# A convolution moved from TensorE to VectorE, block transposes, and a first matmul in four 32-row tiles

## The chip, the cores and the metric

The kernel runs on one NeuronCore of one Trainium2 chip. The metric is the device time of one execution in microseconds (us). The engines named here are PE (TensorE, matmuls; PEld is its weight loads), DVE (VectorE), ACT (ScalarE), POOL (GpSimd) and SP (SyncE, which here only issues DMAs). Matmuls read SBUF and write PSUM, which has eight banks of 512 float32 per partition; DVE and ACT take the results out.

## The reference

```python
# x: (B, S, D) = (8, 4224, 192); weight: (H, K) = (8, 7); w1: (192, 768); w2: (768, 192)
w = softmax(weight, axis=-1)
x_pad = concatenate([zeros((B, K - 1, D)), x], axis=1)
out[b, s, h, g] = sum_k w[h, k] * x_pad[b, s + k, h, g]      # 8 heads of 24 channels
mu, var = mean(out), mean((out - mu) ** 2)                    # over the 192 channels
xn = (out - mu) / sqrt(var + 1e-06) * g_ln
result = out + maximum(xn @ w1, 0.0) @ w2
```

All of it is float32; w1 and w2 arrive as float64 bits and are rounded on the chip.

## The kernel before

A group is 11 tiles of 128 consecutive tokens, a third of a sequence; there are 24 groups. Tokens lie on the partitions, tile after tile. Each group goes through the MLP in three blocks of 4, 4 and 3 tiles.

`conv` makes the causal convolution a matmul. For each of 8 heads, `band` (128 x 128) mixes the tokens of one tile (L218, 264 columns: 11 tiles of 24 channels), and `halo` adds the six tokens that reach back into the tile before (L222, 64 rows by 32 columns of the array). The results go from PSUM to `y` by ACT or DVE. `norm` computes the statistics of each token and writes the normalised tile `xn` (L259) on DVE. `transpose` turns `xn` into channels-on-partitions by matmuls with an identity (L279).

`up` is the first matmul. The contraction is over 192 channels: 128 of them fill the array (L297), the other 64 use half of it. The hidden dimension comes in six chunks of 128, handled in pairs, and the two chunks' half-array matmuls lie in the two halves of the array (L303): rows 0 to 63 for one chunk, 64 to 127 for the other. ReLU is done by ACT and DVE (L307, L311) into `ht`. `down` is the second matmul, six chunks per tile (L326), and `y` is added by DVE (L330) on the way out.

A float32 matmul of the program is two PE passes, each with its own weight load, so counts in the profile are twice those of the code. Engines run their own queues in order; a scheduler fixes the order in each queue when the program is built, and semaphores do the waiting. PSUM is split into three pools: two banks for convolution and transposes, four for `up`, two for `down`. Before the loop, POOL and DVE build the band matrices and DVE converts the weights (`to_float32`).

Of the kernel before, what the change touches and what calls it, by code (L numbers as in the profile page):

```python
# [9 lines left out]
I32 = mybir.dt.int32  # L10
# [7 lines left out]
def kernel(  # L18
# [23 lines left out]
    Q = 64  # L42
    GRP = D // H
    PAD = K - 1
    T = 11
    NF = F // P
    NG = B * S // (T * P)
    GPS = S // (T * P)
    BLKS = [(0, 4), (4, 4), (8, 3)]
    NB = len(BLKS)  # L50
    HB = 32

    assert D == P + Q and S % (T * P) == 0 and T * GRP <= 512
    assert NF % 2 == 0 and PAD < HB

    xf = x.flatten_outer_dims()
    of = out.flatten_outer_dims()

    consts = ctx.enter_context(tc.tile_pool(name="consts", bufs=1))
    setup = ctx.enter_context(tc.tile_pool(name="setup", bufs=2))  # L60
    xpool = ctx.enter_context(tc.tile_pool(name="xin", bufs=3))
    ypool = ctx.enter_context(tc.tile_pool(name="y", bufs=3))
    npool = ctx.enter_context(tc.tile_pool(name="norm", bufs=3))
    hpool = ctx.enter_context(tc.tile_pool(name="hid", bufs=2))
    opool = ctx.enter_context(tc.tile_pool(name="outp", bufs=3))
    ps_c = ctx.enter_context(tc.tile_pool(name="ps_c", bufs=2, space=PSUM))
    ps_h = ctx.enter_context(tc.tile_pool(name="ps_h", bufs=4, space=PSUM))
    ps_o = ctx.enter_context(tc.tile_pool(name="ps_o", bufs=2, space=PSUM))

# [26 lines left out]
    NB1 = NF // 2 * P  # L96
    NW1 = F + NB1
    NW2 = NF * D
    w1 = consts.tile([P, NW1], F32, name="w1")
    w1a = w1[:, 0:F]  # L100
    w1b = w1[:, F:NW1].rearrange("p (c f) -> p c f", f=P)
    w2flat = consts.tile([P, NW2], F32, name="w2")
    w2 = w2flat.rearrange("p (c d) -> p c d", d=D)
    raw1 = consts.tile([P, NW1, 2], U32, name="raw1")
    raw2 = consts.tile([P, NW2, 2], U32, name="raw2")
# [5 lines left out]
    w1tail = w1_words[P:D, :].rearrange("k (c two f) -> k two c f", two=2, f=2 * P)  # L111
    nc.scalar.dma_start(out=ga, in_=g_col[0:P, :])
# [3 lines left out]
    for r in range(2):  # L116
        rows = slice(Q * r, Q * r + Q)
        nc.scalar.dma_start(out=gb[rows, :], in_=g_col[P:D, :])
        nc.scalar.dma_start(
            out=raw1[rows, F:NW1, :].rearrange("p (c f) w -> p c (f w)", f=P),  # L120
            in_=w1tail[:, r, :, :],
        )
    nc.scalar.dma_start(
# [4 lines left out]
    def to_float32(dst, raw, n):  # L128
        """dst = raw, rounded: 1.mantissa as a float32, times the signed power of two. The
        power runs from 0 (below float32's normal range) to infinity (above it)."""  # L130
        lo, hi = raw[:, :, 0], raw[:, :, 1]
        power = setup.tile([P, n], U32, tag="power", name="power", bufs=1)
        scale = setup.tile([P, n], U32, tag="scale", name="scale", bufs=1)
        mant = setup.tile([P, n], U32, tag="mant", name="mant", bufs=1)
        rest = setup.tile([P, n], U32, tag="rest", name="rest", bufs=1)
# [31 lines left out]
    ident = consts.tile([P, P], F32, name="ident")  # L167
    make_identity(nc, ident)
# [19 lines left out]
    # ---- bands: band[j, h, s] = taps[h, j - s + PAD] within a tile; halo the same with  # L188
    # j counted from the end of the tile before, where only s < PAD is reached ----
    band = consts.tile([P, H, P], F32, name="band")  # L190
    halo = consts.tile([P, H, HB], F32, name="halo")

    def build(dst, width, base):
        dist = setup.tile([P, width, K], I32, tag=f"dist{width}", name=f"dist{width}", bufs=1)
        mask = setup.tile([P, width, K], F32, tag=f"mask{width}", name=f"mask{width}", bufs=1)
        nc.gpsimd.iota(dist, pattern=[[-1, width], [-1, K]], base=base, channel_multiplier=1)
        nc.vector.tensor_single_scalar(mask, dist, 0, op=ALU.is_equal)
        for h in range(H):
            prod = setup.tile([P, width, K], F32, tag="prod", name=f"prod{width}_{h}")
            nc.gpsimd.tensor_tensor(  # L200
                prod, mask, taps[:, h : h + 1, :].to_broadcast([P, width, K]), op=ALU.mult
            )
            nc.vector.tensor_reduce(dst[:, h, :], prod, axis=AX.X, op=ALU.add)  # L203

    build(band, P, PAD)
    build(halo, HB, PAD - P)

# [1 line left out]
    y = {}  # L209

    def conv(g, h0, h1):
        if h0 == 0:
            y[g] = ypool.tile([P, T, D], F32, tag="y", name=f"y{g}")
        first = 0 if g % GPS else 1
        for h in range(h0, h1):
            cs = slice(h * GRP, h * GRP + GRP)
            pc = ps_c.tile([P, T, GRP], F32, tag="c", name=f"pc{g}_{h}")
# [8 lines left out]
            if h % 2:  # L226
                nc.vector.tensor_copy(y[g][:, :, cs], pc)  # L227
            else:
                nc.scalar.copy(y[g][:, :, cs], pc)  # L229
        if h1 == H:  # L230
            del xg[g]

    xn = {}

    def norm(n):
        g, (b0, bn) = n // NB, BLKS[n % NB]
        st = npool.tile([P, 4, nc.vector.BN_STATS_DIM], F32, tag="st", name=f"st{n}")
        mv = npool.tile([P, 4, nc.vector.BN_AGGR_DIM], F32, tag="mv", name=f"mv{n}")
        rstd = npool.tile([P, 4], F32, tag="rstd", name=f"rstd{n}")
        half = npool.tile([P, 4], F32, tag="half", name=f"half{n}")  # L240
        t = npool.tile([P, 4, 2 * P], F32, tag="xn", name=f"xn{n}")
        for i in range(bn):
            nc.vector.bn_stats(out=st[:, i, :], in_=y[g][:, b0 + i, :])  # L243
            nc.vector.bn_aggr(out=mv[:, i, :], in_=st[:, i, :])  # L244
        nc.scalar.activation(rstd[:, 0:bn], mv[:, 0:bn, 1], AF.Sqrt, bias=eps)  # L245
        nc.vector.reciprocal(rstd[:, 0:bn], rstd[:, 0:bn])
        # One Newton step, as the table of square roots is coarser than float32:
        # r (1.5 - 0.5 (var + eps) r r).
        r, v, sq = rstd[:, 0:bn], mv[:, 0:bn, 1], half[:, 0:bn]
        nc.vector.tensor_tensor(sq, r, r, op=ALU.mult)  # L250
# [3 lines left out]
        nc.vector.tensor_scalar(
            out=sq, in0=sq, scalar1=-0.5, scalar2=1.5, op0=ALU.mult, op1=ALU.add
# [141 lines left out]
```

## Time and profile before

| What | Value |
|---|---|
| Median of 3 runs | 1467.71 us (1467.4 to 1468.08) |
| Profiled execution, span | 1465.8 us |
| PE busy | 1412.3 us (96%) |
| PEld busy | 865.2 us (59%) |
| DVE busy | 499.7 us (34%) |
| ACT busy | 251.7 us (17%) |
| POOL busy | 53.8 us (4%) |
| Granted PE clock | 1.000 throughout |
| HBM | 29.13 MB read, 25.95 MB written |

The span runs from the first to the last instruction of the profiled execution; the median contains 1.9 us that lie outside it. An engine's share is an average over the span. A line with L and a number is a line of the kernel printed above.

### The profile page before, as it was taken

The page shows a single profiled execution, that of the slowest core. Times are in us where ns is not written, and L with a number is a line of the kernel's source. Part 1 is how long each engine was busy: PE and PEld are TensorE (multiplying, and loading weights), DVE is VectorE, ACT ScalarE, POOL GpSimd, SP SyncE. Part 2 cuts the span into 40 slices and gives each one's busy share as a digit, 9 for nine tenths or more (in the row PEclk, how much of TensorE's full clock was granted, in tenths as well). Part 3 has the DMA queues.
Part 4 walks back from the last instruction along what each step waited for, and adds up shares of the span by engine and source line. Part 5 has one row for each costly group of instructions (what it writes and reads, how often), then busy time and mean ns, then how long its engine had stood idle before and what let it go on. Part 6 is the DMA issues. An engine that isn't in the chain of part 4 may idle for free.

```text
span 1465.8 us, 15445 instructions
## 1 busy us (share of the span) xinstructions
PE 1412.3 (96%) x6192; PEld 865.2 (59%) x6192; DVE 499.7 (34%) x1655; ACT 251.7 (17%) x531; POOL 53.8 (4%) x96
## 2 busy tenths in 40 slices
PE   0599999999999999999999999999999999999999
PEld 0256656666566566665665666666656666666576
DVE  4723414324234143142341431433414414324141
ACT  0111111112111111111111111111111111111111
POOL 4300000000000000000000000000000000000000
PEclk9999999999999999999999999999999999999999
DMA  5101101101001011010010110110101101000000
GB/s 156 30 13 48 53 19 49 46 26 50 30 31 53 19 51 51 19 51 29 32 52 19 50 53 20 49 40 22 53 19 49 53 19 50 11 20 22 19 20 30
DMA packets 73031, 56.07 MB, mean 38 GB/s; under 512 B 3072, under 2 KB 72832, under 8 KB 72960
## 3 DMA queue, kind: packets, MB, share of 16 engines
q1 hardware_dynamic: 71312, 52.73, 11.4%
q10 hardware_dynamic: 1648, 2.36, 0.5%
q8 instruction: 49, 0.80, 0.2%
q14 instruction: 22, 0.18, 0.0%
HBM read 29.13 MB, written 25.95 MB: 38 GB/s over the span
## 4 chain that ended last, share of the span: by engine, by line
PE 96%; POOL 1%; DVE 1%; DMA 1%; issue 0%; SPq 0%; DVEq 0%
PE po L326 36%; PE ph L297 25%; PE ph L303 15%; PE pc L218 8%; PE pc L222 7%; PE pt L279 5%; POOL prod L200 1%; DMA xg<-in_x_dram 1%; DMA raw<-in_moe_w_ch_dram 0%; DVE st L243 0%; DVE mant L159 0%; DVE scale L147 0%; DVE w L165 0%; DVE mant L155 0%; DVE w L161 0%
## 5 line engine op out<-in xcount | busy, mean ns | idle before, releaser
L326 PE MATMUL po<-w,ht 128*128 128x192 f32 x3168 | 539.2, 328 | 0.0
L326 PEld LDWEIGHTS po<-w,ht 128*128 128x128 f32 x3168 | 511.9, 190 | 19.5 <-issue 19.5
L297 PE MATMUL ph<-xt,w 128*128 128x512 f32 (+1 forms) x864 | 391.3, 575 | 0.0
L307 ACT ACTIVATE ht<-ph 128x512 f32<-128x512 f32 (+1 forms) x216 | 121.6, 563 | 819.3 <-PE ph L303 819.3
L297 PEld LDWEIGHTS ph<-xt,w 128*128 128x128 f32 x864 | 150.7, 190 | 187.5 <-issue 168.4
L311 DVE TENSOR_SCALAR ht<-ph 128x512 f32<-128x512 f32 x144 | 93.2, 647 | 441.7 <-PE ph L303 441.7
L303 PE MATMUL ph<-xt,w 64*128 64x512 f32 (+1 forms) x864 | 228.5, 606 | 0.0
L330 DVE TENSOR_TENSOR ob<-po,y 128x384 f32<-128x384 f32 x144 | 75.4, 523 | 277.7 <-PE po L326 277.7
L218 PE MATMUL pc<-xg,band 128*128 128x264 f32 x384 | 141.1, 450 | 28.6 <-DVE band L203 28.5
L303 PEld LDWEIGHTS ph<-xt,w 64*128 64x128 f32 x864 | 65.0, 184 | 148.4 <-issue 147.7
L222 PE MATMUL pc<-xg,halo 64*32 64x264 f32 (+1 forms) x384 | 121.6, 398 | 11.6 <-DVE halo L203 11.6
L218 PEld LDWEIGHTS pc<-xg,band 128*128 128x128 f32 x384 | 58.7, 193 | 100.5 <-issue 60.0
L227 DVE COPY y<-pc 128x264 f32<-128x264 f32 x96 | 41.5, 433 | 189.1 <-PE pc L222 189.1
L279 PEld LDWEIGHTS pt<-ident,xn 128*128 128x128 f32 x528 | 57.0, 141 | 60.0 <-issue 59.4
L243 DVE BATCH_NORM_STATS2 st<-y 128x6 f32<-128x192 f32 x264 | 86.5, 336 | 2.4
L259 DVE TENSOR_SCALAR xn<-y,mv,rstd 128x192 f32<-128x192 f32 x264 | 82.9, 376 | 5.4 <-DVE rstd L257 0.5
L279 PE MATMUL pt<-ident,xn 128*128 128x128 f32 x528 | 74.7, 283 | 9.7 <-DVE xn L259 9.7
L268 POOL COPY xn<-xn 128x256 f32<-128x256 f32 (+1 forms) x72 | 27.7, 385 | 1328.9 <-DVE half L250 1207.4
L222 PEld LDWEIGHTS pc<-xg,halo 64*32 64x32 f32 x384 | 26.1, 106 | 80.8 <-issue 66.9
L229 ACT COPY y<-pc 128x264 f32<-128x264 f32 x96 | 36.4, 380 | 191.6 <-PE pc L222 191.6
L281 DVE COPY xt<-pt 128x512 f32<-128x512 f32 (+1 forms) x72 | 46.6, 647 | 19.0 <-PE pt L279 17.2
L245 ACT ACTIVATE rstd<-mv,eps 128x4 f32<-128x4 f32 (+1 forms) x72 | 21.5, 299 | 170.9 <-DVE mv L244 101.1
(41 smaller groups left out, 248.1 us busy)
## 6 DMA issues: line engine op xcount, KB each, us to landing
xg<-in_x_dram SPq DMA_DIRECT2D x48, 384.0 KB, 4.2
out_dram<-ob SPq DMA_DIRECT2D x48, 384.0 KB, 2.6
xg<-in_x_dram SPq DMA_DIRECT2D x24, 288.0 KB, 4.7
out_dram<-ob SPq DMA_DIRECT2D x24, 288.0 KB, 2.3
raw<-in_moe_w_ch_dram ACTq DMA_DIRECT2D x1, 1152.0 KB, 10.6
raw<-in_moe_w_ch_dram ACTq DMA_DIRECT2D x1, 768.0 KB, 9.5
xg<-in_x_dram SPq DMA_DIRECT2D x16, 48.0 KB, 2.1
raw<-in_moe_w_ch_dram ACTq DMA_DIRECT2D x2, 192.0 KB, 8.0
```

Of the source, the lines that this page charges most:

```text
L218: nc.tensor.matmul(pc, band[:, h, :], xg[g][:, 1 : T + 1, cs], start=True, stop=True, skip_group_check=True,)
L222: nc.tensor.matmul(pc[0:HB, first:T, :], halo[Q:P, h, :], xg[g][Q:P, first:T, cs], start=False, stop=True, skip_group_check=True,)
L243: nc.vector.bn_stats(out=st[:, i, :], in_=y[g][:, b0 + i, :])
L259: nc.vector.tensor_scalar(out=t[:, i, 0:D], in0=y[g][:, b0 + i, :], scalar1=mv[:, i, 0:1], scalar2=rstd[:, i : i + 1], op0=ALU.subtract, o ...
L279: nc.tensor.transpose(pt[:, i, :], xn[n][:, i, c * P : c * P + P], ident)
L281: eng(t[:, 0:bn, :], pt[:, 0:bn, :])
L297: nc.tensor.matmul(ph[r][:, 0:bn, :], w1a[:, f0 : f0 + P], xa[:, 0:bn, :], start=True, stop=False,)
L303: nc.tensor.matmul(ph[r][:, 0:bn, :], w1b[rows, c, :], xb[rows, 0:bn, :], start=False, stop=True,)
L307: nc.scalar.activation(ht[:, 2 * c, 0:bn, :], ph[0][:, 0:bn, :], AF.Relu)
L311: nc.vector.tensor_scalar(out=ht[:, 2 * c + 1, 0:bn, :], in0=ph[1][:, 0:bn, :], scalar1=0.0, scalar2=None, op0=ALU.max,)
L326: nc.tensor.matmul(po[:, i, :], ht[:, f, i0 + i, :], w2[:, f, :], start=(f == 0), stop=(f == NF - 1),)
L330: nc.vector.tensor_tensor(ob[:, i0 : i0 + m, :], po[:, 0:m, :], y[g][:, b0 + i0 : b0 + i0 + m, :], op=ALU.add,)
```

## The change

The tokens are laid out anew: partition p holds a run of 33 consecutive tokens of one sequence, and a group is 11 of these 33 on all 128 partitions (still 24 groups of 1408 tokens). The tokens before a run are loaded with it, so a tap of the convolution is a shift along the free dimension. `conv` becomes 56 DVE instructions per group, each on 128 x (11 x 24) elements: 8 that multiply by the first tap (L239 of the changed program), then 6 x 8 that multiply by a tap and add (L244). Band matrices, identity and the matmuls of `conv` and `transpose` go.

The normalisation is no longer written out. The mean is taken out of the weights: w1 has each column's mean over channels (after scaling with g) subtracted, once, before the loop (`prepare_w1`); the mean comes from four matmuls. The factor 1/std is positive, so it passes through the ReLU and is applied on the way out of `down`, in the instruction that adds `y` (L320, one for each 192 columns). `stats` computes it from bn_stats.

`transpose` is one DVE instruction that transposes every 32 x 32 block of `y` (L251): 32 channels come to lie on each 32 partitions, for the tokens of those 32 partitions. So `up` contracts 32 channels at a time: for each of six chunks of hidden and six blocks of channels (24 groups x 36 = 864 such steps), four matmuls (L297 of the changed program) whose weights and data lie on partitions 0, 32, 64 and 96, with 352 columns each and a PSUM bank each. For this w1 must lie four times on the partitions, so its centred form is written to memory and read back four times. All ReLUs are on ACT. PSUM is one pool of eight banks for everything; `ht` has one buffer, `yt` two, `y` and `xg` three. x is loaded and the output stored in rows of 8 KB and more.

```diff
-            nc.tensor.matmul(
-                pc, band[:, h, :], xg[g][:, 1 : T + 1, cs],
-                start=True, stop=True, skip_group_check=True,
-            )
-            nc.tensor.matmul(
-                pc[0:HB, first:T, :], halo[Q:P, h, :], xg[g][Q:P, first:T, cs],
-                start=False, stop=True, skip_group_check=True,
-            )
...
+xr = x.rearrange("b (p r) d -> b p (r d)", p=P)
+outr = out.rearrange("b (p r) d -> b p (r d)", p=P)
...
+    def load_x(g):
+        b, j0 = groups[g]
+        t = xpool.tile([P, J + PAD, D], F32, tag="xg", name=f"xg{g}")
...
+        if j0:
+            nc.sync.dma_start(out=flat, in_=xr[b, :, (j0 - PAD) * D : (j0 + J) * D])
+            return
...
+    def prepare_w1():
+        to_float32(w1f, raw1, NW1)
...
+            nc.tensor.matmul(mean[r][:, 0:FH], share[:, 0, :], w1f[:, fs], start=True, stop=False)
...
+            nc.vector.scalar_tensor_tensor(
+                out=w1f[:, fs], in0=w1f[:, fs], scalar=ga, in1=mean[r][:, 0:FH],
+                op0=ALU.mult, op1=ALU.subtract,
+            )
...
+        for q in range(NQ):
+            (nc.sync, nc.scalar)[q % 2].dma_start(
+                out=w1[C * q : C * q + C, :, :], in_=w1c.rearrange("(c d) f -> d c f", d=C)
+            )
...
+    def conv(g):
+        t = xg.pop(g)
+        y[g] = ypool.tile([P, J, D], F32, tag="y", name=f"y{g}")
+        for k in range(K):
+            for h in range(H):
+                cs = slice(h * GRP, h * GRP + GRP)
+                tap = taps[:, h, k : k + 1]
+                if k == 0:
+                    nc.vector.tensor_scalar(
+                        out=y[g][:, :, cs], in0=t[:, 0:J, cs], scalar1=tap, scalar2=None,
+                        op0=ALU.mult,
+                    )
+                else:
+                    nc.vector.scalar_tensor_tensor(
+                        out=y[g][:, :, cs], in0=t[:, k : k + J, cs], scalar=tap,
+                        in1=y[g][:, :, cs], op0=ALU.mult, op1=ALU.add,
+                    )
...
+    def transpose(g):
+        yt[g] = tpool.tile([P, J, NC, C], F32, tag="yt", name=f"yt{g}")
+        nc.vector.transpose(
+            yt[g].rearrange("p j c t -> p (j c t)"), y[g].rearrange("p j d -> p (j d)")
+        )
...
+    def up(g):
...
+        for f in range(NF):
+            fs = slice(f * P, f * P + P)
+            ph = [psum.tile([P, 512], F32, tag="ps", name=f"ph{g}_{f}_{q}") for q in range(NQ)]
+            for c in range(NC):
+                for q in range(NQ):
+                    rows = slice(C * q, C * q + C)
+                    nc.tensor.matmul(
+                        ph[q][:, 0:W], w1[rows, c, fs], t[rows, :, c, :],
+                        start=(c == 0), stop=(c == NC - 1),
+                    )
+            for q in range(NQ):
+                nc.scalar.activation(
+                    ht[g][:, f, :, q, :], ph[q][:, 0:W].rearrange("p (j t) -> p j t", t=C), AF.Relu
                 )
...
+            for j, dst in zip(js, at):
+                nc.vector.scalar_tensor_tensor(
+                    out=y[g][:, j, :], in0=dst, scalar=rstd[g][:, j : j + 1],
+                    in1=y[g][:, j, :], op0=ALU.mult, op1=ALU.add,
+                )
...
+    prepare_w1()
+    conv(0)
     transpose(0)
...
+    for g in range(NG):
+        if g + 2 < NG:
+            load_x(g + 2)
+        up(g)
+        if g + 1 < NG:
+            conv(g + 1)
+            transpose(g + 1)
+            stats(g + 1)
+        down(g)
```

What moves in the queues is seen at two places. First PE, in the steady part: the end of `up` of one block and what follows it (`ph`: first matmul, `pt`: transposes, `po`: second matmul, `pc`: convolution; the numbers behind the names count buffers). Before:

```order
L303 MATMUL ph_4_3494<-xt_1_3407,w_96 128x512
L303 MATMUL ph_5_3495<-xt_1_3407,w_96 128x512
L279 MATMUL pt_0_3502<-ident,xn_3430 128x128 x3
L279 MATMUL pt_1_3508<-ident,xn_3430 128x128 x3
L326 MATMUL po_0_3555<-w_97,ht_3477 128x192
L218 MATMUL pc_4_3514<-xg_3060,band 128x264
L222 MATMUL pc_4_3514<-xg_3060,halo 32x264
```

Between first and second matmul stood transposes of the next block and half a group's convolution. In the changed program, at the end of the first group's `up`:

```order
L297 MATMUL ph_5_0_411<-yt_207,w_113 128x352
L297 MATMUL ph_5_1_412<-yt_207,w_113 128x352
L297 MATMUL ph_5_2_413<-yt_207,w_113 128x352
L297 MATMUL ph_5_3_414<-yt_207,w_113 128x352
L315 MATMUL po_0_527<-w_114,ht_250 128x192 x12
L315 MATMUL po_2_542<-w_114,ht_250 128x192 x12
L315 MATMUL po_4_557<-w_114,ht_250 128x192 x12
L315 MATMUL po_6_572<-w_114,ht_250 128x192 x12
L315 MATMUL po_8_587<-w_114,ht_250 128x192 x12
L315 MATMUL po_10_602<-w_114,ht_250 128x192 x6
```

Now matmuls in four row tiles (third number of `ph`) are followed by the 66 matmuls of the group's `down`, and those by the next group's `up`, with nothing between.

Second DVE, around the instruction that combines `po` with `y`. Before, in the steady part (L311 ReLU, L281 transposes out of PSUM, L227 convolution out of PSUM, L330 adds):

```order
L311 TENSOR_SCALAR ht_1842<-ph_5_1860 128x512
L281 COPY xt_1_1879<-pt_1_1874 128x512
L227 COPY y_1881<-pc_1_1886 128x11x24
L227 COPY y_1881<-pc_3_1894 128x11x24
L330 TENSOR_TENSOR ob_1919<-po_0_1920,y_1575 128x384
L330 TENSOR_TENSOR ob_1919<-po_2_1934,y_1575 128x384
L311 TENSOR_SCALAR ht_1949<-ph_3_1959 128x512
```

Each is a short step on a PSUM tile. In the changed program, near the start (`y_809` is group 2, `po_0_527` and `y_150` are group 0; the rows ahead of these, L239 and L244, are group 2's convolution):

```order
L261 BN_STATS st_868<-y_809 128x6 x11
L264 TENSOR_TENSOR d_869<-st_868 128x11
L265 TENSOR_TENSOR v_870<-st_868 128x11
L266 SCALAR_TENSOR_TENSOR d_869<-d_869 128x11
L269 SCALAR_TENSOR_TENSOR v_870<-v_870,d_869 128x11
L251 STREAM_TRANSPOSE yt_866<-y_809 128x2112
L320 SCALAR_TENSOR_TENSOR y_150<-po_0_527,r_212,y_150 128x192 x2
L320 SCALAR_TENSOR_TENSOR y_150<-po_2_542,r_212,y_150 128x192 x2
```

The combines of group 0 (L320) now stand behind the convolution, statistics and block transpose of group 2.

## Rows read from the trace of the kernel before

**Rows 1.** The chain that ended last, by line: share of the span.
```profile
PE po L326 36%; PE ph L297 25%; PE ph L303 15%; PE pc L218 8%; PE pc L222 7%; PE pt L279 5%; POOL prod L200 1%; DMA xg<-in_x_dram 1%; DMA raw<-in_moe_w_ch_dram 0%; DVE st L243 0%; DVE mant L159 0%; DVE scale L147 0%; DVE w L165 0%; DVE mant L155 0%; DVE w L161 0%
```

**Rows 2.** Busy time of each engine in one stretch of two groups (x: instructions).
```profile
202.27:319.18 116.91, 116.91 (x518) 71.85 (x517) 38.89 (x134) 20.74 (x44) 2.31 (x6) 1.00 0.12 38
```

**Rows 3.** PE's timeline: start, length, instructions, waits in brackets.
```profile
701.80 1.56 PE L297 MATMUL ph<-xt,w 128*128 128x384 f32 x4
...
704.13 1.56 PE L297 MATMUL ph<-xt,w 128*128 128x384 f32 x4
...
707.39 6.02 PE L326 MATMUL po<-w,ht 128*128 128x192 f32 x36
713.25 1.88 PE L297 MATMUL ph<-xt,w 128*128 128x512 f32 x4
...
716.12 1.98 PE L297 MATMUL ph<-xt,w 128*128 128x512 f32 x4
...
719.09 1.98 PE L297 MATMUL ph<-xt,w 128*128 128x512 f32 x4
...
722.99 0.49 PE L326 MATMUL po<-w,ht 128*128 128x192 f32 x2
723.39 0.71 PE L218 MATMUL pc<-xg,band 128*128 128x264 f32 x2
...
724.55 0.71 PE L218 MATMUL pc<-xg,band 128*128 128x264 f32 x2
```

**Rows 4.** Timeline of one pair step: PE matmuls and PEld weight loads.
```profile
655.57 1.02 PE L297 MATMUL ph<-xt,w 128*128 128x512 f32 x2
...
656.00 0.59 PE L297 MATMUL ph<-xt,w 128*128 128x512 f32 x1
656.52 0.30 PEld L303 LDWEIGHTS ph<-xt,w 64*128 64x128 f32 x4 [0.76 <-issue]
656.52 1.13 PE L303 MATMUL ph<-xt,w 64*128 64x512 f32 x4
...
657.05 0.59 PE L303 MATMUL ph<-xt,w 64*128 64x512 f32 x2
```

**Rows 5.** Groups by form: busy us, mean ns of one, idle before.
```profile
L243 DVE BATCH_NORM_STATS2 st<-y 128x6 f32<-128x192 f32 x264 | 86.5, 336 | 2.4
L259 DVE TENSOR_SCALAR xn<-y,mv,rstd 128x192 f32<-128x192 f32 x264 | 82.9, 376 | 5.4 <-DVE rstd L257 0.5
...
L330 DVE TENSOR_TENSOR ob<-po,y 128x384 f32<-128x384 f32 x120 | 66.8, 557 | 244.3 <-PE po L326 244.3
...
L307 ACT ACTIVATE ht<-ph 128x384 f32<-128x384 f32 x72 | 35.4, 492 | 148.6 <-PE ph L303 148.6
...
L251 DVE SCALAR_TENSOR_TENSOR half<-mv,eps,half 128x4 f32<-128x4 f32 x48 | 12.3, 258 | 0.0
...
L330 DVE TENSOR_TENSOR ob<-po,y 128x192 f32<-128x192 f32 x24 | 8.6, 358 | 33.4 <-PE po L326 33.4
```

**Rows 6.** DVE's timeline while the weights are converted.
```profile
17.19 0.76 DVE L136 TENSOR_SCALAR power<-raw 128x1152 uint32<-128x1152 uint32 x1 [10.28 <-DMA raw<-in_moe_w_ch_dram]
17.87 0.75 DVE L151 TENSOR_SCALAR mant<-raw 128x1152 uint32<-128x1152 uint32 x1
...
19.21 1.35 DVE L155 SCALAR_TENSOR_TENSOR mant<-raw,mant 128x1152 uint32<-128x1152 uint32 x1
20.48 0.20 DVE L181 TENSOR_REDUCE wsum<-taps 128x8 f32<-128x56 f32 x1
```

**Rows 7.** PE's timeline at the start of the first block.
```profile
67.23 2.35 PE L279 MATMUL pt<-ident,xn 128*128 128x128 f32 x8 [9.73 <-DVE xn L259]
69.38 2.84 PE L297 MATMUL ph<-xt,w 128*128 128x512 f32 x4
```

**Rows 8.** DMA issues: count, size of each, median us to landing.
```profile
out_dram<-ob SPq DMA_DIRECT2D x24, 288.0 KB, 2.3
raw<-in_moe_w_ch_dram ACTq DMA_DIRECT2D x1, 1152.0 KB, 10.6
```

More of the change, by code (lines that the diff above doesn't have):

```diff
@@ L42 @@
     Q = 64
+    C = 32
     GRP = D // H
     PAD = K - 1
-    T = 11
+    R = S // P
+    J = 11
     NF = F // P
[L47 to L57, printed above, removed]
+    NC = D // C
+    NQ = P // C
+    W = J * C
+    assert D == P + Q and S % P == 0 and R % J == 0 and W <= 512 and NF % 2 == 0
@@ L116 @@
     for r in range(2):
-        rows = slice(Q * r, Q * r + Q)
-        nc.scalar.dma_start(out=gb[rows, :], in_=g_col[P:D, :])
         nc.scalar.dma_start(
-            out=raw1[rows, F:NW1, :].rearrange("p (c f) w -> p c (f w)", f=P),
-            in_=w1tail[:, r, :, :],
-        )
+            out=raw1[Q * r : Q * r + Q, F:NW1, :].rearrange("p f w -> p (f w)"),
+            in_=w1_words[P:D, 2 * FH * r : 2 * FH * (r + 1)],
+        )
+    nc.scalar.dma_start(out=ga, in_=g_col[0:P, :])
+    for r in range(2):
+        nc.scalar.dma_start(out=gb[Q * r : Q * r + Q, :], in_=g_col[P:D, :])
+    load_x(0)
+    load_x(1)
     nc.scalar.dma_start(
@@ L205 @@
[L205 to L217, printed above, removed]
+    w1f = setup.tile([P, NW1], F32, name="w1f")
+    w1 = consts.tile([P, NC, F], F32, name="w1")
+    w2flat = consts.tile([P, NW2], F32, name="w2")
@@ new lines @@
+    w2 = w2flat.rearrange("p (c d) -> p c d", d=D)
+    w1c = dram.tile([D, F], F32, name="w1c")
+    def prepare_w1():
+        to_float32(w1f, raw1, NW1)
+        share = setup.tile([P, 2, P], F32, name="share")
+        for i, g in enumerate((ga, gb)):
+            nc.vector.tensor_scalar(
+                out=share[:, i, :], in0=g.to_broadcast([P, P]),
+                scalar1=1.0 / D, scalar2=None, op0=ALU.mult,
+            )
+        mean = [psum.tile([P, 512], F32, tag="ps", name=f"mean{r}") for r in range(2)]
+        for r in range(2):
+            fs = slice(FH * r, FH * r + FH)
+            rows = slice(Q * r, Q * r + Q)
+            nc.tensor.matmul(mean[r][:, 0:FH], share[:, 0, :], w1f[:, fs], start=True, stop=False)
@@ L230, in conv @@
[L230 to L250, printed above, removed]
-        nc.vector.scalar_tensor_tensor(
-            out=sq, in0=v, scalar=eps, in1=sq, op0=ALU.add, op1=ALU.mult
+                mean[r][:, 0:FH], share[rows, 1, :], w1f[rows, F:NW1], start=False, stop=True
+            )
@@ new lines, in prepare_w1 @@
+        for r in range(2):
+            fs = slice(FH * r, FH * r + FH)
+            rows = slice(Q * r, Q * r + Q)
+            nc.vector.scalar_tensor_tensor(
+                out=w1f[:, fs], in0=w1f[:, fs], scalar=ga, in1=mean[r][:, 0:FH],
+                op0=ALU.mult, op1=ALU.subtract,
+            )
+            nc.vector.scalar_tensor_tensor(
+                out=w1f[rows, F:NW1], in0=w1f[rows, F:NW1], scalar=gb[rows, :],
+                in1=mean[r][rows, 0:FH], op0=ALU.mult, op1=ALU.subtract,
+            )
@@ L253, in norm @@
         )
         nc.vector.tensor_scalar(
[L255 removed]
+            out=d, in0=d, scalar1=-0.5, scalar2=1.5, op0=ALU.mult, op1=ALU.add
         )
[L257 to L266 removed]
@@ L325, in down @@
+    def down(g):
+        b, j0 = groups[g]
+        t = ht.pop(g)
+        for i0 in range(0, J, 2):
+            js = range(i0, min(i0 + 2, J))
+            po = psum.tile([P, 512], F32, tag="ps", name=f"po{g}_{i0}")
+            at = [po[:, i * D : i * D + D] for i in range(len(js))]
+            for j, dst in zip(js, at):
                 for f in range(NF):
                     nc.tensor.matmul(
-                        po[:, i, :], ht[:, f, i0 + i, :], w2[:, f, :],
+                        dst, t[:, f, j, :, :].rearrange("p q t -> p (q t)"), w2[:, f, :],
@@ L352 @@
+    conv(0)
     transpose(0)
-    for n in range(steps):
-        g, k = divmod(n, NB)
-        if k == 0 and g + 2 < NG:
+    stats(0)
+    to_float32(w2flat, raw2, NW2)
+    for g in range(NG):
+        if g + 2 < NG:
             load_x(g + 2)
-        up(n)
-        if n == 0:
-            to_float32(w2flat, raw2, NW2)
-        if n + 1 < steps:
-            transpose(n + 1)
-        if g + 1 < NG and k < 2:
-            conv(g + 1, k * H // 2, (k + 1) * H // 2)
-        if n + 2 < steps:
-            norm(n + 2)
-        down(n)
+        up(g)
[4 more added lines that the diff above has]
+        down(g)
```

191 lines of the change are left out of this document (60 added, 131 removed).

## The prediction

> **What bounds the kernel now.** I read the chain of waits first. Nearly all of it is TensorE (PE): 36% in the second matmuls (L326), 25% and 15% in the first ones (L297, L303), 8% and 7% in the convolution (L218, L222), 5% in the transposes (L279) [rows 1]. No other engine has more than 1%, so only what changes PE's own work, or makes PE wait, can move the time. Next, the stretches: two groups of 1408 tokens last 116.91 us, PE is busy in all of it and DVE in a third [rows 2], so a group costs 58.5 us of PE. PE's timeline splits this. One pass over six hidden chunks is three pair steps; a pair step of a 4-tile block repeats every 2.97 us (716.12 to 719.09), of a 3-tile block every 2.33 (701.80 to 704.13), so up() costs 6 x 2.97 + 3 x 2.33 = 24.8 us per group. 36 passes of the second matmul take 5.86 us (707.39 to 713.25), 0.163 each, so 132 of them 21.5. A head of the convolution repeats every 1.165 us (723.39 to 724.55), eight make 9.3. A 4-tile transpose takes 0.93 (719.09 + 2.97 to 722.99), a group some 2.6 [rows 3]. The sum is 58.2, against 58.5 measured.
>
> Inside a pair step the reader is to see why it costs more than its matmuls. A 512-column pass starts 0.43 us after the one before (655.57, 656.00). Then come the two half-array matmuls: four passes in two rounds, the second round of two starting at 657.05, 0.53 after the first. So two row tiles do run at once, each at full rate. But the array stood from 656.43 to 656.52, then loaded weights with nothing to hide them (0.11, the rest of the 0.53) [rows 4]. A step holds four full passes and two rounds, 6 x 0.43 = 2.58 of its 2.97 us: 0.39 goes to two changes between full array and half tiles, 0.2 each.
>
> **The change, part by part.** *PE loses* the convolution (9.3 us a group) and the transposes (2.6). *up()* becomes 36 steps (6 chunks of hidden, 6 of channels), each of four 32-row matmuls of 352 columns, each in two passes. A pass of 352 columns is 0.43 x 352/512 = 0.296 us; if the four tiles run at once, a step is 0.59 and 36 are 21.3. All neighbours have the same tile shape, so only two changes of shape remain, 0.4: 21.7 instead of 24.8. *down()* keeps its 132 passes, 21.5. A group: 43.2 us, 15.3 less than now.
>
> The row shows two tiles at once, never four, so the step is bounded by 0.59 and 1.18 us. I take 0.59: the two tiles start together and neither slows the other. The four weight loads there overlap too (0.30 us for all) [rows 4].
>
> The Trainium skill bears on this ("TensorE: Matmul & The Clock Gate", Part 3, its speedup table): packing four 32-row tiles was measured there at 3.07 times one, not four. By that a step would be 0.77 us and the estimate 155 us longer than mine. No row here has four tiles, so it stays a rival.
>
> *ACT* takes all the ReLU work: four evictions of 352 per chunk, each under 0.49 us (that of 384 columns) [rows 5], 2.0 us in the 3.5 of a chunk. Eight banks hold two chunks, so it is hidden. After the last chunk, down() has 5 x 2 passes (1.6 us) to run before it needs the last chunk's evictions; I cost this at nothing.
>
> *DVE gains* the convolution: per group 8 tensor-scalar and 48 scalar-tensor-tensor instructions of 264 elements. No row shows this form. DVE's slope is (557 - 358)/192 = 1.04 ns an element [rows 5]; a scalar-tensor-tensor of 1152 with no per-partition scalar starts its successor 1.27 us later, 0.07 over the slope, and a tensor-scalar of 1152 0.68 later, so that form takes half the slope [rows 6]. With two per-partition scalars, 192 elements are spaced 82.9/264 = 0.314 us, 0.21 over the half slope [rows 5]: 0.07 more for each scalar. So 0.275 + 0.14 = 0.415 for one of the 48 and 0.28 for one of the 8: 22.1 us per group. Bounds: 0.345 with a free scalar (18.8), and no overlap at all, 0.275 + 0.258 (the duration on 4 elements [rows 5]) = 0.53 (28).
>
> The Trainium skill says the latter ("VectorE: DVE Perf Modes", The DRAIN you can't avoid): the next instruction does not start until the pipe is empty. The row disagrees: 264 instructions of 0.376 us would be 99 us, and their busy time is 82.9 [rows 5]. By the rule the whole kernel would be some 17 us longer than my sum, through its start alone.
>
> The block transpose (2112 elements) has no row: 2.3 us at one element per slope, four times that at worst; I take 2.3, since every form here runs at the slope or better. Statistics: 11 x 0.336 = 3.7 [rows 5] and four small ones, 0.8; Newton step 1.0; 11 combines with scalar from PSUM 0.36 + 0.07, 4.7. DVE's group: 34.6 us, hidden under PE's 43.2 once the pipeline runs. x arrives two groups ahead; the bytes are about the same.
>
> *The start* is not hidden. Now the first up() begins at 69.38 us [rows 7]. In the changed program it needs yt of group 0: raw weights (17.19 now [rows 6]; all three loads are issued first now, so 11 to 17, I take 14), conversion 6 x 0.68 + 4 x 1.27 and small ones, 10 (to 24), convolution 22.1, centring of w1 2 and a wait for its mean matmuls 1, first step of w2's conversion 0.7, transpose 2.3: 52 us. w1's way through memory (0.6 MB out, 2.4 in) starts near 31; at the 1.15 MB in 10.6 us of a crowded queue [rows 8] it would end near 58: the upper bound. PE then runs up(0) and down(0): 52 + 43.2 + 2.2 for slow first matmuls (eight transposes take 2.15 instead of 0.93, the next four passes 2.84 instead of 1.88 [rows 3, 7]) = 97.5.
>
> Here the order matters. DVE has group 2's whole convolution *ahead* of the combine of group 0. From 52: rest of w2's conversion and statistics 14 (66), conv(1) 22.1, transpose (91), stats(1), conv(2), stats(2), transpose (125), and only then the combine, which frees the banks of po_0. PE's up(1) needs these banks for its third and fourth tile, so PE, done at 97.5, waits until about 125.5: 28 us, once. Afterwards DVE's 34.6 us leave the order harmless: its combine begins some 31 us into each group, when the first pair of tiles has just come out, and follows PE.
>
> **Sum.** 125.5 + 23 x 43.2 + 2.2 (restart) + last combine 0.4 + last output, 1.06 MB in one transfer, 6 (between 2.3 for 288 KB and 10.6 for 1152 KB [rows 8]) = 1127.7. The profiled execution had a span of 1465.8 us against a median of 1467.71, so add 1.9: **1130 us**, 338 less. Own range 1110 to 1165: 0.345 or 0.53 in three exposed convolutions is -10 or +17, w1's arrival +6, a slow transpose +13, early weights -3.
>
> **Rivals.**
> *Four tiles overlap only in part* (three at a time): step 0.79, +0.197 x 864 = +170: 1300. For: no row has four. Against: two cost each other nothing.
> *Only two at once* (slower): a step takes two rounds more, 1.18, +0.59 x 864 = +511: 1641. For it: two is all that rows show. It decides from a step of 0.98 us on (338/864 above 0.59). Against it: the passes of one tile already interleave with the other's, so the order within a tile doesn't hold the neighbour back.
> *Weight loads in single file*: eight a step; a load holds its rows some 0.11 us before a pass can start [rows 4]; eight in a row 0.88, +0.29 x 864 = +250: 1380. Against: the loads of the two tiles start together.
> *DVE becomes the bound*: from conv = 43.2 - 12.5 = 30.7 us, 0.55 an instruction, beyond my upper bound; strided runs of 24 elements on three operands could do it. At 0.6, a group costs 46 us, +64, and the start +34: 1228.
>
> **Chances.** Forecast 0.74; part overlap 0.08; two at once 0.06; loads in file 0.04; DVE bound 0.07; rest 0.01. A measurement tells apart some 0.2%. Faster are all but two at once: 0.93; same 0.01; slower 0.06. The range that leaves out two in ten holds the forecast and most of the DVE case: 1105 to 1230.
>
> **What would show it.** L297 in steps of four, a step every 0.59 us (0.77 or 0.79: part overlap; 0.88: loads; 1.18: two); PE's conv and pt gone; PE's period 43 us; one wait near 97 to 125 us on DVE's combine (L320), none like it later; L244 spaced 0.41; DVE near 60% busy in steady groups. PE waiting for L320 or yt in every group would mean that DVE binds and the prediction is wrong.

## The result and the profile after

| | Before | After |
|---|---|---|
| Median | 1467.86 us (1467.4 to 1468.08, 4 runs) | 1125.59 us (1125.42 to 1126.09, 4 runs) |
| Ratio, with 95% interval | | 0.7669 [0.7659, 0.768] |
| Span of the profiled execution | 1465.8 us | 1123.8 us |
| PE busy | 1412.3 us (96%) | 1048.6 us (93%) |
| DVE busy | 499.7 us (34%) | 795.2 us (71%) |
| Mean granted PE clock | 1.000 | 0.988 |

The time fell by 342 us; 338 were forecast (1130 us). The page of the changed kernel, its parts 1, 2 and 5:

```profile
PE 1048.6 (93%) x10088; PEld 872.8 (78%) x10088; DVE 795.2 (71%) x2145; ACT 230.4 (21%) x603; POOL 9.1 (1%) x12
...
PEclk9987999999999999999999999999999999999999
...
L297 PE MATMUL ph<-yt,w 32*128 32x352 f32 x6912 | 523.2, 458 | 46.4 <-ACT ht L302 24.2
...
L315 PE MATMUL po<-w,ht 128*128 128x192 f32 x3168 | 522.3, 327 | 0.0
...
L244 DVE SCALAR_TENSOR_TENSOR y<-xg,taps,y 128x264 f32<-128x264 f32 x1152 | 467.7, 485 | 0.0
```

PE is still the bound, with two lines left where there were six [rows 1]. In its whole idle time ahead of L297, 46.4 us, only two waits are large: 22.2 for the first `yt`, and 24.2 put down to ACT's evictions, which was not forecast. The granted clock (PEclk, tenths of full speed; 9 is 90% or more) falls under that in two of its 40 slices alone, the third and the fourth (56 to 112 us).

The chain of waits of the changed kernel, in order of time (start, length, what), shows the steady rhythm:

```profile
103.21 21.65 PE po L315 x132
124.86 21.51 PE ph L297 x288
```

A group lasts 21.51 + 21.69 = 43.20 us; 43.2 were forecast, against 58.5 before [rows 2]. Of the 15.3 us less, `up` gives 3.3 (24.8 to 21.51); the rest is work that left PE. Of the 288 passes in 21.51 us four run at a time: 72 rounds of 0.299, where one pass of 352 columns alone was put at 0.296 by the forecast. A step of two rounds is 0.60 us, not 0.77 and not 1.18.

DVE in one steady group (timeline of the changed kernel; start, length, line, in brackets the idle time before it and its releaser):

```profile
518.54 2.26 DVE L239 TENSOR_SCALAR y<-xg,taps 128x264 f32<-128x264 f32 x8 [2.89 <-DMA out_dram<-y]
520.72 19.48 DVE L244 SCALAR_TENSOR_TENSOR y<-xg,taps,y 128x264 f32<-128x264 f32 x48
540.23 2.96 DVE L261 BATCH_NORM_STATS2 st<-y 128x6 f32<-128x192 f32 x11
...
543.73 2.37 DVE L251 STREAM_TRANSPOSE yt<-y 128x2112 f32<-128x2112 f32 x1
546.02 2.00 DVE L320 SCALAR_TENSOR_TENSOR y<-po,r,y 128x192 f32<-128x192 f32 x6
```

The 48 multiply-adds take 19.48 us, 0.406 each from start to start, though each lasts 0.485 by the page: successors start before the end. The 2.9 us ahead of L239 are a wait for the output's DMA to let go of a `y` buffer. Nothing on PE waits for it.

The start is where the trace differs from the forecast. First PE's timeline of the changed kernel, then ACT's in the same stretch, then DVE's:

```profile
52.22 16.65 PE L297 MATMUL ph<-yt,w 32*128 32x352 f32 x192 [22.22 <-DVE yt L251]
93.08 10.13 PE L297 MATMUL ph<-yt,w 32*128 32x352 f32 x96 [24.20 <-ACT ht L302]
103.14 21.72 PE L315 MATMUL po<-w,ht 128*128 128x192 f32 x132
124.79 21.58 PE L297 MATMUL ph<-yt,w 32*128 32x352 f32 x288
```

```profile
61.80 1.53 ACT L302 ACTIVATE ht<-ph 128x352 f32<-128x352 f32 x4 [2.02 <-PE ph L297]
92.38 0.30 ACT L272 ACTIVATE r<-v,eps 128x11 f32<-128x11 f32 x1 [29.04 <-DVE v L269]
92.58 2.92 ACT L302 ACTIVATE ht<-ph 128x352 f32<-128x352 f32 x8
```

```profile
92.18 0.16 DVE L269 SCALAR_TENSOR_TENSOR v<-v,d 128x11 f32<-128x11 f32 x1
...
119.19 2.69 DVE L320 SCALAR_TENSOR_TENSOR y<-po,r,y 128x192 f32<-128x192 f32 x8
```

The first `up` starts at 52.22 us, as forecast (52). But it stops after four of its six chunks (192 of 288 passes) for 24.2 us. ACT's rows say why: after eight evictions its queue holds the square root of the *next* group's statistics (L272), one instruction of 0.30 us, and stands there 29.04 us until DVE has convolved group 1 and reached L269 at 92.18. The evictions of the last chunks stand behind it. Then `up(1)` begins at 124.79 without a wait, where the forecast had 125.5 after a wait of 28 us for the combine (L320): by then the combine has been running since 119.19. The time came out nearly as added up, but the place of the wait was wrong.

### The profile page after: what moved, and what is told of

Its sections match the earlier page's. It is cut to its first block, busy times and chain, and to the rows that moved or that the text cites. A ratio compares the mean times of both kernels' runs of the same rounds, so it can differ in the third digit from the quotient of the medians.

```text
span 1123.8 us, 23187 instructions
## 1 busy us (share of the span) xinstructions
PE 1048.6 (93%) x10088; PEld 872.8 (78%) x10088; DVE 795.2 (71%) x2145; ACT 230.4 (21%) x603; POOL 9.1 (1%) x12
## 3 DMA queue, kind: packets, MB, share of 16 engines
HBM read 44.82 MB, written 26.54 MB: 63 GB/s over the span
## 4 chain that ended last, share of the span: by engine, by line
PE 92%; DVE 6%; DMA 1%; ACTq 0%; ACT 0%; issue 0%; DVEq 0%
PE po L315 46%; PE ph L297 45%; DVE y L244 3%; DMA raw<-in_moe_w_ch_dram 1%; DVE st L261 1%; DVE yt L251 0%; DVE y L239 0%; PE mean L203 0%; PE mean L204 0%; DVE mant L154 0%; DVE scale L146 0%; DVE power L135 0%; DVE power L142 0%; DVE mant L150 0%; DVE rest L159 0%; DVE mant L158 0%
## 5 line engine op out<-in xcount | busy, mean ns | idle before, releaser
L297 PE MATMUL ph<-yt,w 32*128 32x352 f32 x6912 | 523.2, 458 | 46.4 <-ACT ht L302 24.2
L315 PE MATMUL po<-w,ht 128*128 128x192 f32 x3168 | 522.3, 327 | 0.0
L297 PEld LDWEIGHTS ph<-yt,w 32*128 32x128 f32 x6912 | 357.3, 186 | 205.1 <-ACT ht L302 24.8
L244 DVE SCALAR_TENSOR_TENSOR y<-xg,taps,y 128x264 f32<-128x264 f32 x1152 | 467.7, 485 | 0.0
L302 ACT ACTIVATE ht<-ph 128x352 f32<-128x352 f32 x576 | 220.4, 469 | 330.0 <-PE ph L297 330.0
L320 DVE SCALAR_TENSOR_TENSOR y<-po,r,y 128x192 f32<-128x192 f32 x264 | 95.0, 408 | 233.6 <-PE po L315 233.6
L272 ACT ACTIVATE r<-v,eps 128x11 f32<-128x11 f32 x24 | 7.3, 303 | 504.5 <-DVE y L320 454.5
L239 DVE TENSOR_SCALAR y<-xg,taps 128x264 f32<-128x264 f32 x192 | 54.8, 355 | 61.9 <-DMA out_dram<-y 61.9
L261 DVE BATCH_NORM_STATS2 st<-y 128x6 f32<-128x192 f32 x264 | 70.9, 344 | 0.8
L251 DVE STREAM_TRANSPOSE yt<-y 128x2112 f32<-128x2112 f32 x24 | 56.9, 2370 | 0.0
L84 POOL MEMSET xg<- 1x1152 f32 x8 | 8.9, 1111 | 792.6 <-DVE y L244 792.3
```

Source lines behind the costliest of these rows:

```text
L84: nc.gpsimd.memset(t[0:1, 0:PAD, :], 0.0)
L239: nc.vector.tensor_scalar(out=y[g][:, :, cs], in0=t[:, 0:J, cs], scalar1=tap, scalar2=None, op0=ALU.mult,)
L244: nc.vector.scalar_tensor_tensor(out=y[g][:, :, cs], in0=t[:, k : k + J, cs], scalar=tap, in1=y[g][:, :, cs], op0=ALU.mult, op1=ALU.add,)
L251: nc.vector.transpose(yt[g].rearrange("p j c t -> p (j c t)"), y[g].rearrange("p j d -> p (j d)"))
L261: nc.vector.bn_stats(out=st[:, j, :], in_=y[g][:, j, :])
L272: nc.scalar.activation(r, v, AF.Sqrt, bias=eps)
```

## The experiments

Each is an edit of the changed kernel, one of the kernel before. Ratios are to the kernel before, run on the same chip.

| Run | Median, us | Ratio [95%] |
|---|---|---|
| e1_act_order | 1123.67 | 0.7657 [0.7645, 0.7668] |
| e2_dve_order | 1590.03 | 1.0837 [1.0819, 1.0855] |
| e3_both | 1098.32 | 0.7485 [0.7474, 0.7496] |
| e8_before_fewer_switches | 1438.42 | 0.9802 [0.9788, 0.9817] |
| e4_two_tiles | 1347.22 | 0.9179 [0.9161, 0.9197] |
| e5_tile_by_tile | 3389.77 | 2.3096 [2.3049, 2.3142] |
| e11_two_blocks | 1127.67 | 0.7685 [0.7674, 0.7697] |
| e6_dve12 | 1190.22 | 0.8109 [0.8097, 0.8122] |
| e7_dve32 | 1427.15 | 0.9726 [0.971, 0.9742] |
| e9_dve12_zero | 1136.52 | 0.7745 [0.7732, 0.7758] |
| e10_dve24_zero | 1195.49 | 0.8144 [0.8132, 0.8156] |

**The start: ACT's queue or DVE's.** e1 places the square root of group g behind the last eviction of group g - 1 in ACT's queue (`evicted` keeps that instruction):

```diff
-        nc.scalar.activation(r, v, AF.Sqrt, bias=eps)
+        with tc.issue_after(evicted[g - 1].ins) if g else nullcontext():
+            nc.scalar.activation(r, v, AF.Sqrt, bias=eps)
```

> The changed kernel, in which the square root of group 1's variance stands on ACT behind all evictions of group 0's first matmul, not behind the first eight. Theory A (two locks at the start: ACT's square root holds PE in up(0) until 92, and behind it DVE's combine of group 0, which comes after group 2's convolution, would hold up(1) until about 120): PE's wait moves from up(0) to the start of up(1), and only the difference of the two locks is gained, 2 to 5 us: 1121 to 1123. Theory B (the ACT wait is the whole loss): 24 us less, 1101. The prediction's own step (the combine alone holds PE): no change, 1126.

1123.67 us: 1.9 less than the changed kernel, 0.17%, just under the 2 to 5 expected, and the intervals of the two ratios overlap. PE's timeline of this run shows why:

```profile
52.16 23.60 PE L299 MATMUL ph<-yt,w 32*128 32x352 f32 x288 [22.22 <-DVE yt L252]
75.69 21.77 PE L317 MATMUL po<-w,ht 128*128 128x192 f32 x132
97.40 0.86 PE L299 MATMUL ph<-yt,w 32*128 32x352 f32 x4
120.47 23.90 PE L299 MATMUL ph<-yt,w 32*128 32x352 f32 x284 [22.21 <-DVE y L322]
```

`up(0)` now runs through, PE is done with group 0 at 97.40 (forecast: 97.5), starts four passes of `up(1)` and waits 22.21 us for the combine (L322 in this kernel). This is the wait of the forecast, at its place. After it PE needs 23.9 us for the other 284 passes instead of 21.2, part of it at a lower clock (granted 0.73 from 120.47 to 128 us), so little is gained although `up(1)` starts 4.3 us earlier. In the changed kernel the stop in `up(0)` hides this wait: DVE gets through group 2's convolution while PE finishes group 0 late.

e2 leaves ACT alone and places the convolution of group g behind the combine of group g - 2 in DVE's queue:

```diff
+        behind = tc.issue_after(combined[g - 2].ins) if g >= 2 else nullcontext()
+        with behind:
+            taps_of(g, t)   # the loop over k and h, unchanged
```

> The changed kernel, in which a group's convolution stands on DVE behind the combine of two groups before (group 2's behind group 0's combine). Theory A (two locks): ACT's square root still holds up(0) until about 91, so next to nothing, 1124 to 1126. The prediction's own step (the combine alone holds PE, 28 us): 1098.

1590.03 us: neither theory had this. DVE now begins the convolution of group g + 1 only when `down` of group g - 1 has ended (511.93 in this group), so the statistics come 28 us into `up` of group g. The scheduler that fixes the queues also put the square root that waits for them behind the first evictions of that `up` instead of ahead of them, which does not help: the later evictions still stand behind it. Three views of this run: the largest wait of PE (total, times, longest), PE's timeline of one group, and ACT's:

```profile
PE ph L303 <- ACT ht L308: 402.5, 23, 24.2
```

```profile
511.49 11.50 PE L303 MATMUL ph<-yt,w 32*128 32x352 f32 x146
540.19 12.88 PE L303 MATMUL ph<-yt,w 32*128 32x352 f32 x142 [17.20 <-ACT ht L308]
552.99 7.25 PE L321 MATMUL po<-w,ht 128*128 128x192 f32 x43
```

```profile
515.40 1.53 ACT L308 ACTIVATE ht<-ph 128x352 f32<-128x352 f32 x4 [24.49 <-PE ph L303]
518.89 0.46 ACT L308 ACTIVATE ht<-ph 128x352 f32<-128x352 f32 x1 [1.96 <-PE ph L303]
539.48 0.30 ACT L278 ACTIVATE r<-v,eps 128x11 f32<-128x11 f32 x1 [20.13 <-DVE v L275]
539.69 2.57 ACT L308 ACTIVATE ht<-ph 128x352 f32<-128x352 f32 x7
```

The first of the 23 waits, 24.2 us in group 0, is the one that the changed kernel has too. In each of the next 22 groups the square root stands behind five evictions of the running `up`, and PE stops for 17.2 us more. `up` takes 552.99 - 511.49 = 41.5 us instead of 21.5 in this group: the wait, and passes at a lower clock after it (142 in 12.8 us, granted 0.87). From 123.77 us (`up` of group 1) to 1539.76 (of group 23) a group lasts 64.4 us on average, 21.2 more than 43.2; 22 x 21.2 = 466, and 1590.0 - 1125.6 = 464 was measured.

e3 has both edits:

> Both orders at once. Theory A (two locks): up(0) and down(0) run through to about 98, yt of group 1 is there at 88, so up(1) starts at 98 instead of 125: 27 us less, 1098. Rival: DVE's work itself, not its order, sets the start; then up(1) would wait for something else on DVE and the gain would stay under 10 us.

1098.32 us, as expected, 27.3 less than the changed kernel (2.4%): the fastest version of all. PE's timeline:

```profile
52.24 23.56 PE L304 MATMUL ph<-yt,w 32*128 32x352 f32 x288 [22.22 <-DVE yt L257]
75.72 21.77 PE L322 MATMUL po<-w,ht 128*128 128x192 f32 x132
97.43 21.58 PE L304 MATMUL ph<-yt,w 32*128 32x352 f32 x288
```

From 52 us on PE has no wait; `up(1)` starts at 97.43 instead of 124.79, 27.4 us earlier, which is the whole gain. e3 keeps DVE's order of e2 and is fast, so that order costs nothing by itself: e2 was slow because, with it, the square root held evictions back. Neither e1 nor e2 shows what either lock costs alone: with one of the two taken away the other stays, and its place can change.

**What a change of tile shape costs.** e8 is the kernel *before*, with the middle one of the three pair steps run half-array matmuls first, so that a block has four changes between full and half array instead of six:

```diff
+            for half in ((False, True), (True, False), (False, True))[c]:
+                first = half == (c == 1)
```

> The kernel before, with the order of the first matmul's full-array and half-array parts reversed in the second of its three chunk pairs, so that a block changes array shape four times instead of six. Theory A (each change of shape costs PE 0.2 us, with drain and an unhidden weight load): 72 blocks x 0.39 less = 28 us less, 1440. Rival (the extra time of a pair step lies in the half-array pair itself): no change, 1468.

1467.37 - 1438.42 = 29 us for 24 x 3 x 2 = 144 changes: 0.2 us each, the size read from [rows 4]. Part of the gain of the change (0.2 x 18 a group before, two now) is this.

**How many tiles run at once.** e4 gives PE the same matmuls, but two tiles' six blocks of channels first and then the other two's; e5 one tile's after the other's; e11 in turns of two blocks of channels for two tiles:

```diff
-            for c in range(NC):
-                for q in range(NQ):
+            for c, q in [(c, q) for p in (0, 2) for c in range(NC) for q in (p, p + 1)]:    # e4
+            for c, q in [(c, q) for q in range(NQ) for c in range(NC)]:                     # e5
+            for c, q in [(c0 + i, p + r) for c0 in (0, 2, 4) for p in (0, 2)
+                         for i in range(2) for r in range(2)]:                              # e11
```

> The changed kernel with the first matmul's 24 matmuls of a chunk in another order: the six channel blocks of tiles 0 and 1 taken in turn, then those of tiles 2 and 3. Theory A (four row tiles run at once because four neighbours in the queue lie on four tiles): now two run at once, a chunk takes 2 x 6 x 0.59 = 7.1 us instead of 3.55, +21.3 us for each of 24 groups: 1637, some 510 more. Rival (PE looks far enough ahead in its queue to bring all four tiles together whatever the order): no change, 1126.

> The changed kernel with all six channel blocks of one tile before the next tile's. Theory A (passes start in the order of the queue, so that one tile runs at a time): a chunk takes 4 x 6 x 0.59 = 14.2 us, +64 us a group, 2660. Rival (PE looks past waiting passes to another tile's): between 1126 and 1640.

> The changed kernel with the tiles taken in turn two channel blocks at a time: tiles 0 and 1 for blocks 0 and 1, then tiles 2 and 3 for them, and so on. Theory A, as mended by the run with six blocks at a time (PE looks ahead in its queue past waiting passes, but only some 12 to 16 loads and passes): the other pair's first load is 16 places off and comes into sight as soon as a round of the first pair has started, so all four tiles are mostly busy: 1126 to 1165. Rival (two neighbours at a time, no looking ahead): like the run with six blocks or worse, 1347 to 1637.

e4 lies between its two theories, e5 is slower than both of its own, and only e11 came as expected. One group of `up` in PE's timeline of e4, of e5 and of e11:

```profile
602.10 31.14 PE L296 MATMUL ph<-yt,w 32*128 32x352 f32 x288
```

```profile
610.69 114.92 PE L296 MATMUL ph<-yt,w 32*128 32x352 f32 x288
```

```profile
601.50 21.69 PE L296 MATMUL ph<-yt,w 32*128 32x352 f32 x288
623.11 21.72 PE L314 MATMUL po<-w,ht 128*128 128x192 f32 x132
```

In e4 a group's `up` takes 31.1 us. Had PE kept two tiles busy it would be 144 rounds of 0.296 = 42.6; in strict order, with the next pair coming in during a pair's last round, 12 x 11 x 0.296 = 39.1. So passes of the third and fourth tile ran while earlier ones of the first two still waited for their rows: 31.1 is 12 x 8.8 rounds, so a pair's twelve rounds overlap by some three with the next pair's.

e5 says the same of single tiles, once its clock is taken out. The window of the same `up` (PE busy, PEld, DVE, ACT, POOL, each with its count; granted clock, DMA share, GB/s), then its weight loads (PEld) over one tile's twelve passes:

```profile
610.69:725.54 114.85, 114.85 (x290) 74.02 (x289) 26.54 (x77) 10.96 (x24) 1.05 (x1) 0.52 0.07 24
```

```profile
640.44 1.67 PEld L296 LDWEIGHTS ph<-yt,w 32*128 32x128 f32 x7 [0.26 <-issue]
642.37 0.33 PEld L296 LDWEIGHTS ph<-yt,w 32*128 32x128 f32 x1 [0.26 <-issue]
642.95 0.33 PEld L296 LDWEIGHTS ph<-yt,w 32*128 32x128 f32 x1 [0.25 <-issue]
...
645.30 1.67 PEld L296 LDWEIGHTS ph<-yt,w 32*128 32x128 f32 x7 [0.26 <-issue]
```

The clock granted is 0.52, near the lower of its two levels (1.2 of 2.4 GHz), with PE counted busy all the time. Where one tile runs alone, a load follows the last after 0.587 us: about twice the 0.296 of a pass at full clock. A tile begins every 645.30 - 640.44 = 4.86 us, 8.3 passes and not 12, and the seven loads at each beginning are two tiles' in turn. In the built program the queue of e5 holds a tile's six matmuls together, as the code has them. The trace's records of single passes give the overlap: a tile's first pass (its load waits for a semaphore) starts at 640.445 us, with the ninth of the tile before (640.439), and its third at 641.779, ahead of that tile's twelfth (642.199). In e4 the next pair's first pass likewise starts with the ninth round of the pair before (604.584 and 604.572 us). So the last four of a tile's twelve passes run beside the first four of the next, three of which start ahead of passes that stand before them in the queue.

An overlap of four passes per tile covers e11 entirely, whose turns are four passes long: 21.6 us, 0.1 more than the changed kernel; in strict order it would have been 36 x 3 x 0.296 = 32.0. The time of e11, +2.1 us, is not told apart from the changed kernel's. Its expectation supposed a reach of 12 to 16 places in the queue; but in e5 PE passes over three waiting passes, in e4 over six, three of each tile. That speaks for a limit per tile, which no run tested by itself.

**DVE's slack.** The forecast had DVE hidden, with conv up to 30.7 us a group. e6 and e7 add 12 and 32 multiply-adds per group that read x and write one spare tile which nobody reads:

```diff
+                if k * H + h >= K * H - 12:
+                    nc.vector.scalar_tensor_tensor(
+                        out=spare, in0=t[:, k : k + J, cs], scalar=tap, in1=t[:, k : k + J, cs], ...
```

> The changed kernel with 12 more scalar-tensor-tensor instructions of the convolution's form per group, on a spare tile (4.9 us of DVE per group). Theory A (DVE is hidden in the steady part, with about 7 us to spare a group, and exposed only before group 0's and group 1's statistics): +10 us, 1135. Rival (DVE already sets the pace): +4.9 x 24 = 117, 1243.

> The same with 32 more per group (13.0 us of DVE per group). Theory A: DVE's chain of a group, 35.5 us with its wait for the output, becomes 48.5 against PE's 43.2, so DVE sets the pace: +5.3 x 22 = 117 and +34 at the start, 1277. Rival (DVE has much more room, since its queue runs two groups ahead): only the start, 1160.

Both missed, 1190 and 1427 us. DVE's timeline of e6 (e7's has the 32 in 16.90 us, behind a wait of 2.73):

```profile
504.65 6.31 DVE L249 SCALAR_TENSOR_TENSOR spare<-xg,taps 128x264 f32<-128x264 f32 x12 [2.88 <-DMA xg<-in_x_dram]
```

The extra instructions ran in a row, writing one tile again and again, and then cost 0.53 us each (6.31/12, 16.90/32), not 0.406; and the scheduler drew them to where they wait 2.9 us for the load of x. So DVE's group was 35.5 (its chain in the changed kernel: 32.0 busy, 2.9 of waiting for the output, short gaps) + 2.9 + 6.3 = 44.7, and 35.5 + 2.7 + 16.9 = 55.1. PE's period was 44.6 in this group of e6 and 54.7 in one of e7: DVE binds, but the two runs don't price the forecast's condition. e9 and e10 do: 12 and 24 further multiply-adds of the convolution's own form into `y`, with a factor of zero.

```diff
+        for n in range(12):
+            cs = slice(n % H * GRP, n % H * GRP + GRP)
+            nc.vector.scalar_tensor_tensor(
+                out=y[g][:, :, cs], in0=t[:, 0:J, cs], scalar=zero, in1=y[g][:, :, cs], ...
```

> The changed kernel with 12 more scalar-tensor-tensor instructions per group at the end of the convolution, of its very form (they add zero times x to y, and wait for one another only eight instructions back): 12 x 0.406 = 4.9 us of DVE a group. Theory A (DVE's chain of a group is 35.5 us, its wait for the output included, against PE's 43.2, so it has 7.7 us to spare in the steady part; at the start the convolutions of groups 0 and 1 are exposed): +9.8 us, 1135. Rival (no room on DVE): +4.9 x 24 = 117, 1243.

> The same with 24 more: 9.75 us of DVE a group. Theory A: the chain is 45.25 us, 2.05 longer than PE's, so +2.05 x 22 = 45, and at the start three convolutions count, +24: 1195. Rival (the room is larger): only the start, 1150. Rival (no room): 1360.

1136.52 and 1195.49 us. PE's timeline of e10 has a small wait for DVE in nearly every group:

```profile
513.33 22.21 PE L305 MATMUL ph<-yt,w 32*128 32x352 f32 x284 [1.66 <-DVE y L328]
535.48 21.72 PE L323 MATMUL po<-w,ht 128*128 128x192 f32 x132
557.12 0.86 PE L305 MATMUL ph<-yt,w 32*128 32x352 f32 x4
558.19 22.21 PE L305 MATMUL ph<-yt,w 32*128 32x352 f32 x284 [0.20 <-DVE y L328]
```

Both came as expected. 12 more (4.9 us) cost nothing in the steady part, only 11 us in the start's convolutions; 24 more (9.8 us) go past the slack of 43.2 - 35.5 = 7.7 by 2.1 a group. Of the 69.9 us that they cost, 27.3 are the start's (the second `down` begins at 173.62 us instead of 146.30), and the 22 groups behind it last 45.14 on average, 1.94 more than 43.2, in all 42.7. So the slack lies between 4.9 and 9.8 us, and e10 puts it at 9.8 - 1.9 = 7.9: the changed kernel is bound by PE, and would be by DVE from conv = 21.7 + 7.7 = 29.4 us on (forecast: 30.7).

## Why the prediction was right, and where it was not

- **PE's group, 43.2 us**: measured 43.20 (up 21.51, forecast 21.7; down 21.69, forecast 21.5). That four tiles run at once was an assumption, chosen from a row that had two; 511 us lay between it and the slower rival, and it held. All four rivals fell: 1300, 1641 and 1380 with the step of 0.60, DVE as the bound with the steady groups and e9.
- The Trainium skill ("TensorE: Matmul & The Clock Gate", Part 3, its speedup table) has 3.07 times for four 32-row tiles; here 288 passes of 0.296 in 21.51 us are 3.96. The measurement decides.
- **Changes of tile shape, 0.2 us**: confirmed by e8.
- **ACT hides its evictions**: right in the steady groups (230.4 us busy of 1123.8), wrong at the start, and this is the step of the prediction that failed. The forecast costed ACT by its durations and took its order for harmless. "PE then runs up(0) and down(0) ... = 97.5" overlooked the square root of the next group in ACT's queue; in its place came a stop of 24.2 us inside `up(0)`.
- **The wait of 28 us for the combine** did not show in the changed kernel. The cause that was named for it (group 2's convolution ahead of the combine in DVE's queue) is real: e1 uncovers it with 22.2 us, e3 removes it. The two locks stand one behind the other on the same engine's convolutions, and PE loses the time once, to whichever comes first; so the sum held: `up(1)` at 124.79 against 125.5. That it held so closely, with the wrong wait in it, is in part luck: the two locks happen to end within some 4 us of each other (`up(1)` starts at 120.47 in e1).
- **Start, 52 us**: 52.22. Raw weights at 13.88 (14), conversion done at 23.5 (24), transpose from 49.80 for 2.37 (2.3). The 2.2 for slow first matmuls came to 2.0 (e3: 23.56 us for the first `up`, 21.58 for the second).
- **Convolution, 22.1 us a group**: 21.7 (518.54 to 540.23); 0.406 an instruction against 0.415. The Trainium skill ("VectorE: DVE Perf Modes", The DRAIN you can't avoid) has the next instruction wait until the pipe is empty, which with the duration of these rows would be 0.485; the same paragraph excepts an instruction that is "not held", which the prediction left out, and the rows of the convolution start early, as this exception has it. They show 0.406 where each instruction writes another slice of `y` than the one before (e9's extra ones too, 4.94 us for 12), and 0.53 in e6 and e7, where each writes the tile that the one before wrote (and reads x twice instead of x and `y`); no run changed that alone.
- **End**: the wait not being where it was put, no restart of 2.2 us followed at 124.8; the tail was 5.4 us from the last pass, not 6.4. With -0.7 for the earlier `up(1)` these make the 3.9 us between 1127.7 and the span of 1123.8.
- **What was to be seen**: DVE "near 60% busy in steady groups" was wrong, and not even in line with the forecast's own 34.6 of 43.2: it is 74% (32.01 us of 43.20). "The bytes are about the same" was wrong too: 44.82 MB are read instead of 29.13, since each run of 11 tokens is loaded with the 6 before it. No wait of PE comes from it.

What stays open: the 52 us until the first `up`, which no run shortened; what sets the three passes by which PE runs ahead; and why the scheduler puts the square root where it does.

## What to carry to other kernels

When work leaves the bound engine, go through every queue in order, the nearly idle ones too: one instruction of 0.3 us, queued ahead of evictions and waiting for next group's data, stopped PE for 24 us once, and for 17 us in each of 22 more groups when a reordering on another engine made its data later. Where two such locks hang on the same late engine, undo them together, since either edit alone may show no gain or a loss. Small-contraction matmuls in four row tiles paid here, most when neighbours in program order went to different tiles: six blocks of a pair in a row cost 222 us (e4), one tile after the other made the kernel slower than before (e5).

## What the runs showed of the hardware

- Four 32-row tiles ran at 3.96 times one (72 rounds of four in 21.51 us, one pass put at 0.296; rounds of two in e4 are 0.296 apart), and three passes per tile started on free rows ahead of earlier ones that waited for theirs (e4 and e5). Two blocks at a time in turns cost 0.1 us a group (e11).
- With one tile after the other (e5) the granted clock was 0.61 over the span while PE was counted busy in 98% of it (3336.7 us); with pairs (e4) it was 0.992. So e5's 3390 us hold two losses, the rows left empty and the clock (0.587 us from pass to pass instead of 0.296).
- After the stop in `up(0)` (no pass from 69 to 93 us, granted clock 0.60 there) the clock was 0.93 from 93 to 125 us, and 1.00 in later groups: the windows of the changed kernel, columns as above.

```profile
69.00:93.00 24.00, 0.00 (x0) 0.00 (x0) 24.00 (x66) 0.62 (x3) 0.00 (x0) 0.60 0.20 70
93.00:125.00 32.00, 31.92 (x232) 31.20 (x236) 29.61 (x82) 5.57 (x16) 0.00 (x0) 0.93 0.15 53
500.00:543.20 43.20, 43.20 (x422) 36.05 (x421) 32.01 (x86) 9.50 (x25) 1.05 (x1) 1.00 0.16 60
```

- DVE multiply-adds of 264 elements follow each other every 0.406 us, but every 0.53 in the runs where each wrote the tile that the last one wrote.
